# Identity products on TensorE in its first idle stretches, in an attention and MLP kernel

## The chip, the cores and the metric

The kernel runs on one core of one Trainium2 chip. The metric is device time in microseconds (us). Three runs of the kernel before gave 598.51, 599.78 and 601.29 us; the median is 599.78 us. One further execution was profiled: it took 598.44 us, of which the span from the first to the last instruction is 596.7 us and 1.7 us lie around it. All rows below come from that execution, and its times count from the start of its span.

## The reference

Attention with rotated queries and keys, then a two-layer MLP whose nonlinearity is a clipped parabola. Cut to what matters:

```python
# q, k, v: (4, 8, 576, 64); w_in: (512, 2048); w_out: (2048, 512); all float32
q_rot, k_rot = rotate(q), rotate(k)          # halves of the 64 turned by cos/sin of the position
scores = q_rot @ k_rot.transpose(0, 1, 3, 2) / 8
attn = exp(scores - max(scores))
attn = attn / (sum(attn) + 1e-9)
x = (attn @ v).transpose(0, 2, 1, 3).reshape(2304, 512)
h = x @ w_in
g = where(h >= 1, h, where(h <= -1, 0, (h + 1) ** 2 / 4))
out = g @ w_out                              # float32
```

## The kernel before

Each float32 operand of a large product is split into two float16 numbers, a high and a low part, after scaling by a power of two that is found at run time from a sum of squares; a product of two such operands is three float16 products. TensorE (PE) does the products, ScalarE (ACT) and VectorE (DVE) scale, split, exponentiate and reduce, SyncE (SP) issues all DMAs. Per batch element there are two blocks of 256 queries; a block runs over four pairs of heads and its scores, softmax, transposes by DMA, products with v and MLP steps are mixed with those of its neighbours.

What sets the order: every step is added to a `Plan` with its engine, and then all steps are issued in the order that the table `ORDER` gives. Each number of it is a position in the list of steps that are still left. Each engine works through its own instructions strictly in that order, so a step that waits holds up all that stand behind it on its engine. Steps on different engines wait for each other where their data ask for it.

The first 20 us, which the change touches, do this for the first batch element:

- `init` lets GpSimd (POOL) write the 128x128 float32 identity `idn` (it lies in the second half of the tile `xT`, by whose name the profile calls it) and then the permutation `prm`.
- k of each pair of heads comes by DMA into `rk`. ACT squares it with a running sum (L249). `root` lets PE add up that sum over the partitions (L255: all ones times one column, into `psV`), from which DVE takes an exponent in five or so tiny instructions (L260, L262, L265, L272).
- DVE turns k and q by the angles (L289, L291). `split_sum` (L318, L319) adds the two terms on PE: `idn` times `rk`, and `prm` times the other buffer (named `w` in the profile), into the two banks `psO`; for q into the bank `psH`. ACT takes the high part out of the bank (L327), PE subtracts it there (L323, with `nd`, a scaled identity), and ACT takes the low part.
- `scores` (L595) writes `psS`; DVE takes the row maximum (L568), ACT the exponential (L570).
- `prep_w` reads the words of w_in and w_out on DVE (L516, L518, L520) as soon as their DMAs have landed; its rest (L547, L548) is on PE.

A float32 product is recorded as two matmuls and two weight loads, so a row of the profile with x2 is one product of the program.

Of the kernel before, what the change touches and what calls it, by code (L numbers as in the profile page):

```python
# [1 line left out]

# [1 line left out]

# [16 lines left out]

ORDER = """
# [58 lines left out]
"""  # L83

PICK = set("""
lo0 lo12 lo15 m1.2 m1.6 m2.0 m2.1 m2.2 m2.3 m2.4 m2.7 m3.0 m3.1 m3.2 m3.3 m3.4 m3.5 m4.0 m4.1 m4.3 m5.2 m5.3
m5.4 m5.5 m6.0 m6.1 m6.2 m6.4 m6.5 m6.6 m6.7 m7.2 m7.4 m7.5 m8.2 m8.4 m8.5 m9.0 m9.1 m9.2 m9.3 v0 v1  # L90
""".split())
O_CHUNKS = 5


class Plan:
# [38 lines left out]
        self.steps.append((eng, cost, at, fn, sorted(deps.items()), f"{self.group} {eng}", bw, turn,  # L134
                           f"{self.group}.{self.part} {eng}", mode, self.alt))

    def order(self):
        left = list(range(len(self.steps)))
        return [self.steps[left.pop(int(k))][3] for k in ORDER.split()]


@with_exitstack
def kernel(
# [12 lines left out]
    nc = tc.nc  # L156
    B, _, NP, S = km.shape[1:]
# [43 lines left out]
    idn = x1[:, 2048:2304].bitcast(F32)  # L201
# [7 lines left out]
    psS = [ps.tile([128, 1024], F32, name=f"psS{i}") for i in range(2)]  # L209
# [637 lines left out]
                      [("xL", l, e, j) for l in range(2) for e in range(2) for j in range(NP)], 128,  # L847
                      [done + span * (m + nst + 0.5) for m in range(4)], left_rows(b - 1))

    order = plan.order()  # L850
    with tc.manual_schedule():
        for fn in order:
            fn()
# [57 lines left out]
```

## Time and profile before

| what | value |
|---|---|
| median of three runs | 599.78 us (598.51 to 601.29) |
| profiled execution | 598.44 us, span 596.7 us |
| PE busy | 564.8 us, 95% of the span |
| DVE busy | 482.3 us, 81% |
| ACT busy | 455.9 us, 76% |
| mean granted clock of PE | 0.991 |
| the chain that ended last, by engine | PE 64%, DVE 15%, ACT 10%, DMA 7%, issue 3%, SP 1% |

How to read it: the shares are averages over stages with different limits. PE is busy nearly all the time from 80 us on, but not in the first 60 us, where DVE and ACT are. A timeline row has the start, the length, the engine, the line of the kernel, the operation, what is written and read, its shape and how many instructions were merged; in brackets the idle time of the engine just before it and who ended it. The clock column is the share of TensorE's full 2.4 GHz that was granted. A matmul's end is modelled, so the spacing of starts tells more than the length.

### The profile page before, as it was taken

The numbers are of one execution on the slowest core, as the hardware profiler recorded it, in microseconds if no ns is written. First come the engines' busy times: TensorE is split into PE (matmuls) and PEld (weight loads), VectorE is DVE, ScalarE is ACT, GpSimd is POOL, SyncE is SP. The second block draws the span as 40 slices with busy tenths as digits, with TensorE's granted clock in tenths as the row PEclk, the third lists the DMA queues.
The fourth block names the chain that finished last, engine by engine and source line by source line (L and its number), as shares of the span: only waits on it lengthen the run. The fifth ranks groups of instructions, "written<-read, shape, count | busy, mean of one in ns | idle before, by whom it ended". The sixth has DMA issues, their size and how long they took to land.

```text
span 596.7 us, 12159 instructions
## 1 busy us (share of the span) xinstructions
PE 564.8 (95%) x4824; PEld 365.1 (61%) x4824; DVE 482.3 (81%) x782; ACT 455.9 (76%) x922; POOL 1.5 (0%) x11
## 2 busy tenths in 40 slices
PE   4758989899999999999999999999999999999996
PEld 3423556556576766666666666666577666676763
DVE  6999999999899999989999788778988765523332
ACT  4999989999899889896957778787887676452431
POOL 1000000000000000000000000000000000000000
PEclk9889989999999999999999999999999999999999
DMA  8999998967986899596856892672557547400001
GB/s 271 337 215 264 242 242 224 286 120 143 224 187 164 157 168 208 103 236 158 178 136 134 189 170 41 110 152 59 120 96 140 75 85 137 98 10 27 1 3 52
DMA packets 184008, 88.94 MB, mean 149 GB/s; under 512 B 170768, under 2 KB 172048, under 8 KB 183952
## 3 DMA queue, kind: packets, MB, share of 16 engines
q1 hardware_dynamic: 183952, 88.17, 66.7%
q8 instruction: 38, 0.62, 0.4%
q14 instruction: 18, 0.15, 0.1%
HBM read 38.60 MB, written 4.72 MB: 73 GB/s over the span
## 4 chain that ended last, share of the span: by engine, by line
PE 64%; DVE 15%; ACT 10%; DMA 7%; issue 3%; SPq 1%; DVEq 0%; ACTq 0%
PE psO L741 25%; PE psH L709 24%; PE psV L630 7%; PE psS L595 5%; DMA pT<-phl 3%; DVE phl L580 3%; DVE sca L568 3%; ACT p L570 2%; ACT phl L578 2%; DMA w<-in_w_out_dram 2%; DVE g L732 1%; PE psO L547 1%; DVE r L728 1%; DMA w<-in_w_in_dram 1%; DMA rk<-in_km_dram 1%
## 5 line engine op out<-in xcount | busy, mean ns | idle before, releaser
L709 PE MATMUL psH<-xT,w 128*128 128x256 f16 (+1 forms) x1920 | 205.3, 262 | 1.2 <-ACT a L717 1.2
L741 PE MATMUL psO<-w,g 128*128 128x512 f16 x864 | 203.4, 379 | 0.0
L709 PEld LDWEIGHTS <-w 128*128 128x128 f16 x1920 | 171.1, 98 | 36.9 <-issue 4.0
L741 PEld LDWEIGHTS <-g 128*128 128x128 f16 x864 | 81.5, 98 | 83.8 <-issue 2.8
L570 ACT ACTIVATE p<-psS,sca 128x576 f32<-128x576 f32 x144 | 105.5, 736 | 29.2 <-DVE sca L568 20.8
L580 DVE SCALAR_TENSOR_TENSOR phl<-p,sca,phl 128x576 f16<-128x576 f32 x144 | 115.8, 812 | 11.5 <-ACT phl L578 11.0
L578 ACT ACTIVATE phl<-p,sca 128x576 f16<-128x576 f32 x144 | 107.8, 770 | 16.0 <-DVE sca L575 11.5
L568 DVE TENSOR_REDUCE sca<-psS 128x1 f32<-128x576 f32 x144 | 105.3, 749 | 8.9 <-PE psS L595 8.1
L732 DVE SCALAR_TENSOR_TENSOR g<-r,g 128x512 f16<-128x512 f32 x72 | 49.4, 686 | 34.9 <-ACT g L730 34.7
L717 ACT ACTIVATE a<-psH 128x512 f32<-128x512 f32 x72 | 42.4, 589 | 41.8 <-PE psH L709 37.9
L728 DVE SCALAR_TENSOR_TENSOR r<-a,r 128x512 f32<-128x512 f32 x72 | 49.4, 686 | 20.3 <-ACT r L726 19.4
L730 ACT ACTIVATE g<-r 128x512 f16<-128x512 f32 x72 | 45.0, 625 | 23.2 <-DVE r L728 13.1
L595 PE MATMUL psS<-kT,qT 64*128 64x512 f16 (+1 forms) x768 | 59.7, 284 | 2.9 <-ACT p L570 2.7
L595 PEld LDWEIGHTS <-qT 64*128 64x128 f16 x768 | 29.2, 94 | 46.6 <-issue 24.2
L630 PE MATMUL psV<-pT,vS 128*64 128x256 f16 (+1 forms) x512 | 42.4, 288 | 1.7 <-DMA pT<-phl 1.7
L630 PEld LDWEIGHTS <-vS 128*64 128x64 f16 x512 | 26.8, 109 | 8.8 <-issue 5.9
L721 DVE SCALAR_TENSOR_TENSOR r<-a 128x512 f32<-128x512 f32 x38 | 26.1, 687 | 6.0 <-ACT a L717 5.2
L570 ACT ACTIVATION_READ_ACCUMULATOR p<-psS,sca 128x1 f32 x144 | 28.6, 199 | 0.0
L630 PE MATMUL psV<-pT,vM 128*64 128x256 f16 (+1 forms) x320 | 25.0, 286 | 0.0
L724 ACT ACTIVATE r<-a 128x512 f32<-128x512 f32 x34 | 21.2, 625 | 4.0 <-DVE g L732 2.1
L726 ACT ACTIVATE r<-r 128x512 f32<-128x512 f32 x34 | 21.3, 627 | 0.6
L644 DVE SCALAR_TENSOR_TENSOR xT<-psV,sca,xT 128x320 f16<-128x320 f32 (+1 forms) x24 | 14.6, 610 | 7.7 <-ACT xT L641 7.7
(108 smaller groups left out, 475.7 us busy)
## 6 DMA issues: line engine op xcount, KB each, us to landing
w<-in_w_in_dram SPq DMA_DIRECT2D x14, 512.0 KB, 6.6
w<-in_w_out_dram SPq DMA_DIRECT2D x12, 512.0 KB, 8.0
rv<-in_vm_dram SPq DMA_DIRECT2D x8, 512.0 KB, 4.5
out_dram<-o SPq DMA_DIRECT2D x16, 256.0 KB, 3.0
dup<-in_km_dram SPq DMA_DIRECT2D x6, 576.0 KB, 6.6
rk<-in_km_dram SPq DMA_DIRECT2D x6, 576.0 KB, 4.5
rq<-in_qb_dram SPq DMA_DIRECT2D x4, 640.0 KB, 5.0
vM<-vS SPq DMA_DIRECT2D x8, 256.0 KB, 5.3
```

The lines of the kernel that those rows point to most:

```text
L568: plan.add("dve", dve_cost(S, psum=True), at, lambda m=m, src=src: nc.vector.tensor_reduce(out=m, in_=src, op=ALU.max, axis=AX.X, negate=T ...
L570: plan.add("act", act_cost(S, psum=True, ptrs=2), at, lambda a=a, e=e, m=m, src=src: nc.scalar.activation(out=p32[e], in_=src, func=AF.Exp ...
L578: plan.add("act", act_cost(S), at, lambda a=a, e=e, hi=hi: nc.scalar.activation(out=hi, in_=p32[e], func=AF.Copy, scale=rr[:, a:a + 1]), r ...
L580: plan.add("dve", dve_cost(S, ptrs=1), at, lambda a=a, e=e, hi=hi, lo=lo: nc.vector.scalar_tensor_tensor(out=lo, in0=p32[e], scalar=rr[:, ...
L595: nc.tensor.matmul(out=psS[a][:, lo:hi], lhsT=qT[hf][d, l, j, c:c + 128], rhs=kT[ks][d, j, m, lo:hi], start=z == 0, stop=z == 2)
L630: nc.tensor.matmul(out=outs[a], lhsT=st, rhs=moving(a, blk), start=z == 0, stop=z == len(seq) - 1)
L709: nc.tensor.matmul(out=psH[:, n * i:n * i + n], lhsT=wi[ft // 2][:, wl, kk, 128 * (ft % 2):128 * (ft % 2) + 128], rhs=xfn(xl, kk), start=z ...
L717: plan.add("act", act_cost(512, psum=True, ptrs=0), at, lambda one=one: nc.scalar.activation(out=a, in_=psH, func=AF.Relu, scale=2.0 ** -7 ...
L728: plan.add("dve", dve_cost(512), at, lambda one=one: nc.vector.scalar_tensor_tensor(out=r, in0=a, scalar=one, in1=r, op0=ALU.max, op1=ALU. ...
L730: plan.add("act", act_cost(512, ptrs=0), at, lambda g=g, one=one: nc.scalar.activation(out=g[:, 0], in_=r, func=AF.Relu, scale=1.0, bias=- ...
L732: plan.add("dve", dve_cost(512), at, lambda g=g, one=one: nc.vector.scalar_tensor_tensor(out=g[:, 1], in0=r, scalar=-one, in1=g[:, 0], op0 ...
L741: nc.tensor.matmul(out=psO[pos[tt]], lhsT=g[:, gl, n * i + 128 * tt:n * i + 128 * tt + 128], rhs=wo[ft // 2][:, wl, ft % 2, :], start=ft = ...
```

## The change

Five entries of a new kind stand in `ORDER`: `*b.n` calls `idle(b, n)`, which issues n products of `idn` with itself into the first 128 columns of a PSUM bank (bank 0 is `psH`, bank 4 the first of `psS`). Nothing reads them; the next real product into that bank starts it anew. There are 7 + 6 + 5 + 7 products into `psH` and 2 into `psS`. All numbers of the table are the same as before and in the same order.

```diff
...
-5 4 4 9 1 2 26 4 1 0 0 75 48 51 25 122 121 98 22 46 70 3 25 21 3 129 128 91 91 1 2 4 3 2 2 17 0 16 13 17 55 31
-32 15 0 51 30 15 12 27 1 0 5 24 5 0 0 3 0 1 0 17 3 3 2 75 35 0 0 207 7 32 11 69 203 14 203 11 67 29 46 1 197 0
...
+5 4 4 *0.7 9 1 2 26 4 1 0 0 75 48 51 25 122 121 98 22 46 70 3 *0.6 25 21 3 129 128 91 91 1 2 4 3 2 2 17 0 16 13
+17 55 31 32 15 0 51 30 15 12 27 *0.5 1 0 5 *0.7 24 5 0 0 3 0 1 0 17 3 3 2 75 35 0 0 *4.2 207 7 32 11 69 203 14
...
-    def order(self):
+    def order(self, idle):
         left = list(range(len(self.steps)))
-        return [self.steps[left.pop(int(k))][3] for k in ORDER.split()]
+        return [partial(idle, *map(int, k[1:].split("."))) if k[0] == "*" else self.steps[left.pop(int(k))][3]
+                for k in ORDER.split()]
...
-    order = plan.order()
+    def idle(b, n):
+        bank = (psH, psO[0], psO[1], psV, psS[0], psS[1])[b]
+        for _ in range(n):
+            nc.tensor.matmul(out=bank[:, 0:128], lhsT=idn, rhs=idn, start=True, stop=True)
+
+    order = plan.order(idle)
...
```

On PE, at the very start of the program, these rows stood in the kernel before (`psV` is the bank of the root sums, `psO` the two banks of k, `xT_78` is `idn`; lines are those of each kernel's own file, 3 higher in the changed one):

```order
L255 MATMUL psV<-sca 128x1 x2
L318 MATMUL psO_107<-rk,xT_78 128x288
L319 MATMUL psO_107<-w,prm 128x288
L318 MATMUL psO_108<-rk,xT_78 128x288
L319 MATMUL psO_108<-w,prm 128x288
L255 MATMUL psV<-sca 128x1
L318 MATMUL psH<-rq_86,xT_78 128x256
L319 MATMUL psH<-w,prm 128x256
```

And these stand there now:

```order
L856 MATMUL psH<-xT_78 128x128 x7
L258 MATMUL psV<-sca 128x1
L856 MATMUL psH<-xT_78 128x128 x6
L258 MATMUL psV<-sca 128x1
L856 MATMUL psH<-xT_78 128x128 x5
L321 MATMUL psO_107<-rk,xT_78 128x288
L322 MATMUL psO_107<-w,prm 128x288
L321 MATMUL psO_108<-rk,xT_78 128x288
L322 MATMUL psO_108<-w,prm 128x288
L856 MATMUL psH<-xT_78 128x128 x7
L258 MATMUL psV<-sca 128x1
L321 MATMUL psH<-rq_86,xT_78 128x256
```

So four batches stand ahead of the first, the second and the third root sum and of the first k products; no real instruction has moved against another.

On PE, a little later, ahead of the first scores (`psS_103` is the first score bank, `nd_99` the scaled identity of q), the kernel before had:

```order
L323 MATMUL psH<-qT_64,nd_99 128x256
L595 LDWEIGHTS qT_64
L595 MATMUL psS_103<-kT_62,qT_64 128x512
```

And now:

```order
L326 MATMUL psH<-qT_64,nd_99 128x256
L856 MATMUL psS_103<-xT_78 128x128 x2
L598 LDWEIGHTS qT_64
L598 MATMUL psS_103<-kT_62,qT_64 128x512
```

The fifth batch stands between the subtraction of q and the first score product. The instructions of DVE, ACT, POOL and SP and their order are the same in both kernels.

## Rows read from the trace of the kernel before

**Rows 1.** The page's 40 slices: busy tenths of PE, DVE and ACT.

```profile
PE   4758989899999999999999999999999999999996
...
DVE  6999999999899999989999788778988765523332
ACT  4999989999899889896957778787887676452431
```

**Rows 2.** Chain that ended last, first 60 us: start us, us, what.

```profile
4.03 5.17 DMA rk<-in_km_dram
9.22 10.67 DMA w<-in_w_out_dram
...
19.99 0.69 DVE o L516
...
41.10 2.08 PE psO L547 x2
```

**Rows 3.** Timeline of PE.

```profile
5.87 0.59 PE L255 MATMUL psV<-sca 128*128 128x1 f32 x2 [5.87 <-ACT w L249]
7.78 0.59 PE L255 MATMUL psV<-sca 128*128 128x1 f32 x2 [1.32 <-ACT w L249]
9.42 1.30 PE L318 MATMUL psO<-rk,xT 128*128 128x288 f32 x2 [1.05 <-DVE sca L262]
...
11.47 1.17 PE L318 MATMUL psO<-rk,xT 128*128 128x288 f32 x2
12.43 1.17 PE L319 MATMUL psO<-w,prm 128*128 128x288 f32 x2
13.39 0.33 PE L255 MATMUL psV<-sca 128*128 128x1 f32 x2
...
14.10 0.59 PE L319 MATMUL psH<-w,prm 128*128 128x256 f32 x2
...
14.78 0.28 PE L255 MATMUL psV<-sca 128*128 128x1 f32 x2
...
16.04 0.85 PE L595 MATMUL psS<-kT,qT 64*128 64x512 f16 x10 [0.19 <-ACT kT L327]
...
17.41 0.65 PE L319 MATMUL psO<-w,prm 128*128 128x288 f32 x2
17.89 0.65 PE L318 MATMUL psO<-rk,xT 128*128 128x288 f32 x2
```

**Rows 4.** Timeline of DVE.

```profile
8.40 0.16 DVE L260 TENSOR_REDUCE sca<-psV 128x1 f32<-128x1 f32 x1
...
12.71 0.42 DVE L291 TENSOR_TENSOR rq<-rq,rt 128x256 f32<-128x256 f32 x1
...
15.03 0.69 DVE L516 TENSOR_SCALAR xT<-w 128x1024 uint32<-128x1024 uint32 x1 [0.31 <-DMA w<-in_w_in_dram]
...
16.92 0.76 DVE L568 TENSOR_REDUCE sca<-psS 128x1 f32<-128x576 f32 x1
...
19.99 0.69 DVE L516 TENSOR_SCALAR o<-w 128x1024 uint32<-128x1024 uint32 x1 [0.33 <-DMA w<-in_w_out_dram]
...
44.98 0.69 DVE L516 TENSOR_SCALAR o<-w 128x1024 uint32<-128x1024 uint32 x1 [1.41 <-PE psO L547]
```

**Rows 5.** Timeline of ACT.

```profile
13.63 0.50 ACT L327 ACTIVATE kT<-psO,sca 128x288 f16<-128x288 f32 x1 [1.06 <-PE psO L319]
14.73 0.47 ACT L327 ACTIVATE qT<-psH,sca 128x256 f16<-128x256 f32 x1 [0.60 <-PE psH L319]
...
17.71 0.74 ACT L570 ACTIVATE p<-psS,sca 128x576 f32<-128x576 f32 x1
```

**Rows 6.** Timeline of POOL: the identity.

```profile
1.01 0.29 POOL masks.py:199 TENSOR_SCALAR_AFFINE_SELECT xT<-xT 128x128 f32<-128x128 f32 x1
```

**Rows 7.** Timeline of the weight loads (PEld).

```profile
17.17 0.43 PEld L319 LDWEIGHTS psO<-w,prm 128*128 128x128 f32 x2
```

**Rows 8.** Stretches: busy of PE, PEld, DVE, ACT, POOL; PEclk, DMA share, GB/s.

```profile
10.00:13.40 3.40, 3.40 (x9) 2.37 (x8) 3.40 (x11) 2.53 (x7) 0.00 (x0) 1.00 0.99 331
...
25.00:27.20 2.20, 2.20 (x6) 1.47 (x6) 2.20 (x5) 2.01 (x8) 0.00 (x0) 0.51 0.99 331
...
40.50:44.20 3.70, 3.10 (x5) 1.35 (x6) 3.07 (x4) 3.38 (x9) 0.00 (x0) 0.54 1.24 246
```

More of the change, by code (lines that the diff above doesn't have):

```diff
@@ L1 @@
 from contextlib import ExitStack
+from functools import partial
 import numpy as np
```

112 rows, old and new, of the table ORDER are left out of this document.

## The prediction, made before the changed kernel ran

> **What bounds the kernel now.** I read the slices of the page first [rows 1]: PE is full only from about the sixth slice on (15 us each), while DVE is full from the second. So the first 60 us, where the change lies, are not PE's. Next the chain that ended last [rows 2]: it opens with the DMA that brings k (4.03 to 9.20 us), goes on with the DMA that brings w_out (9.22 to 19.89), and passes to DVE at 19.99, which waited for just that DMA. PE is not on it before 41.10 us. Then the timelines of PE, DVE and ACT beside each other [rows 3 to 5], to see who would notice a faster or a later PE in the first 20 us.
>
> PE runs there at its low rate at first. The product L318 or L319 of 288 columns starts 0.96 us after the one ahead at 11.47 and 12.43, and 0.48 us at 17.41 and 17.89 [rows 3]; the root sum L255 takes 0.59 us at 5.87 and 7.78, 0.28 us at 14.78. The granted clock reads 1.00 for 10.0 to 13.4 us [rows 8], which the doubled spacing contradicts, so for the start I go by the spacing: 1.2 GHz until about 13.4 us, 2.4 GHz after. Ahead of that rise PE had worked without a break since 9.42, 4.0 us; the two short root sums ahead of it lifted nothing. Two later falls are in the record (0.51 in 25.0 to 27.2, 0.54 in 40.5 to 44.2), and the second of these ended after 3.1 us of work in 3.7 [rows 8].
>
> **The change part by part.** No real instruction moves, and no engine but PE gets any. What is added is 27 products on PE, and what may go is the low rate from about 6 to 13.4 us.
>
> *Price of one product.* It is not in the trace. By columns, 128 of 288 of the nearest product give 0.96 x 128/288 = 0.43 us at the low rate and 0.48 x 128/288 = 0.21 at the high [rows 3]. The other end is that its two weight loads hide under nothing: L255, with one column, is hardly more than those loads, so 0.59 + 0.43 = 1.02 and 0.28 + 0.21 = 0.49. I take the lower end, because in the stream of float32 products the loads of L319 (17.17, 0.43 us) begin before its first column at 17.41 [rows 3, 7]. Less than the columns it cannot be.
>
> *Batch 1 (7).* It waits for the identity, ready at 1.01 + 0.29 = 1.30 [rows 6]. 7 x 0.43 = 3.0 us, done at 4.3. The root sum behind it waits for ACT until 5.87 in any case [rows 3]: 1.6 us of cover. Cost 0.
>
> *Batch 2 (6).* If PE has its high rate by then: the root sum is done at 5.87 + 0.28 = 6.15, the batch at 6.15 + 6 x 0.21 = 7.4, and the second root sum starts at 7.78 as before, on ACT [rows 3]. Cost 0, with 0.4 us of cover. Behind this batch stands the result for DVE's L260 at 8.40 [rows 4], which got it 0.03 us ahead of need (7.78 + 0.59 = 8.37); DVE is in order, so a later root sum holds all of DVE.
>
> *Batch 3 (5).* 8.06 + 1.07 = 9.1, ahead of 9.42, when DVE frees the first k product. Cost 0.
>
> *The four k products.* 4 x 0.48 = 1.9 instead of 4.0 us: they end at 11.35 instead of 13.39.
>
> *Batch 4 (7).* 11.35 + 1.5 = 12.85; the third root sum is done at 13.1 (before: 13.39 + 0.33). Turned q is there at 12.71 + 0.42 = 13.13 [rows 4], so the two products of q end at 13.13 + 0.43 + 0.59 = 14.15 (0.43 is 256 columns at the high rate) instead of 14.10 + 0.59 = 14.69. So 1.5 us of the 2.0 won go to the batch and to DVE.
>
> *Batch 5 (2).* 0.43 us between q and the scores. These ended at 16.04 + 0.85 = 16.89 [rows 3]; with q 0.54 earlier and the batch in full they end at 16.78, so DVE's maximum at 16.92 is not held. Cost 0, with 0.1 us of cover.
>
> *Who takes the gain.* ACT waits 1.06 us for k at 13.63 and 0.60 us for q at 14.73 [rows 5]; 1.06 and 0.54 of that go. But ACT's first exponential at 17.71 follows DVE's row maximum at 16.92 + 0.76, and DVE comes to that maximum straight from work that began at 15.03, when the DMA of w_in had landed [rows 4]. ACT would then idle about 1.6 us ahead of 17.71 instead of ahead of 13.63 and 14.73. At 19.99 DVE waits for the DMA of w_out, the chain's second link [rows 2, 4]. Nothing of a faster PE reaches 20 us, and from there on DVE, ACT and PE have what they had. The sum is 598.44 + 0 = 598.4 us.
>
> By the Trainium skill, "TensorE: Matmul & The Clock Gate", section "Terms", the penalty of a throttled clock is the throttled time times the share of pulses that is missing. For the k products alone that would give the 2.0 us back at the end, 596.4 us. The rows do not agree: the stretch is off the chain, so that rule prices PE's time and not the kernel's.
>
> *Against the median.* The profiled execution is 1.34 us under the median of the three runs, which lie 2.8 us apart. If part of that spread is the moment at which the rate rises at the start, the change narrows it; I can't show it from one trace and go half the way: 599.1 us.
>
> **The rivals.**
>
> *A. The first batch does not lift the rate.* Then batch 2 runs at 1.2 GHz: 6.46 + 6 x 0.43 = 9.0, the second root sum is done at 9.6, and DVE's L260 at 8.40 waits 1.2 us. From here it decides: any root sum done after 8.40 costs DVE time. If the rate rises after 4.0 us of work from 5.87 on, at 9.9, batch 3 ends at 10.8, the k products at 12.75, batch 4 at 14.25, the third root sum at 14.5, q at 15.55, 0.85 late; with batch 5 in full (0.43) the scores end at 16.89 + 1.28 = 18.2, 1.25 us after DVE wants them. 0.33 us of it vanish in the wait at 19.99 [rows 4]: + 0.9, 599.4 us. If only work without root sums lifts it (9.6 + 4.0 = 13.6), q ends 2.7 us late and the sum is + 2.8, 601.2 us. For it: batch 1 gives 3.0 us of work, a little less than what stood ahead of either rise in the rows. Against it: 3.1 us were enough once [rows 8].
>
> *B. The products' loads do not hide.* Price 1.02 and 0.49. With the rate up after 4.1 us, batch 1 ends at 6.9 (4 x 1.02 + 3 x 0.49), the second root sum at 10.4, batch 3 at 12.8, the k products at 14.75, batch 4 at 18.2, q at 19.5: 4.8 late, with batch 5 5.8 at the scores, less 0.33: + 5.5, 603.9 us. Against it stand rows 7.
>
> *C. PE's gain does pass.* If the order of DVE and ACT bends so that their 1.06 + 0.54 us count, 596.8 us. If besides the low rate at 40.5 to 44.2 falls away, on which DVE waits 1.41 us at 44.98 [rows 4, 8], 595.4 us. Against it: DVE waits for DMAs at 15.03 and 19.99, and what PE does at 37 to 41 us is set by ACT and DVE, which the change leaves as they are. The rule of the Trainium skill named above would put this rival at 596.4 us.
>
> **How the numbers follow.** My forecast 0.66, A 0.20, B 0.05, C 0.09. The time is that of the forecast, 599.1 us. The three runs tell a difference of about 0.5%, 3.0 us, from no change: under 596.8 is faster, over 602.8 slower. Faster is half of C and little else, 0.05; slower is B and a slow tail of A, 0.06; within is the rest, 0.89. For 8 in 10 the range takes the forecast with the spread of the runs, most of A and the near end of C: 597.2 to 601.8; B, the far end of C and the late end of A with a high run stay out.
>
> **What would show it.** Right: products 0.21 to 0.43 us apart; the k products 0.48 apart from about 9.4 on; the second root sum no later than 8.40; the third at 12.8; ACT with a new idle time of about 1.6 us ahead of its first exponential near 17.7; DVE still waiting for w_in near 15.0 and for w_out near 20.0; all rows after 20 us where they were. Wrong: DVE waiting for PE at L260 or at its first L568 (A, B); or DVE at L516 earlier than 19.9 (C). A change of more than 3 us with the first 20 us unmoved would mean that the later falls of the rate are set by something that I have not seen.

## The result

The changed kernel took 603.67 us (median of 9 runs, 601.04 to 604.29) against 600.17 us of the kernel before (9 runs, 598.07 to 601.29): a ratio of 1.0052, 95% interval 1.0036 to 1.0067. It is slower by about half a percent: 3.1 us by the ratio, while the medians lie 3.5 us apart. Three executions of 969 us or more, one each of e9, e11 and e12, are left out of the ratios below, but not out of the medians. I had forecast 599.1 us and no difference that can be told. The profiled execution took 604.29 us with a span of 602.5, against 598.44 and 596.7 before: 5.8 us, more than the typical 3.1, so this trace shows the loss in its larger form.

Lines of the changed file are 3 higher: L258 is the root sum, L263 its reduce on DVE, L321 and L322 the k and q products, L571 the row maximum, L519 the first step on a raw weight, L856 the identity products.

The timeline of PE in the changed kernel, where [rows 3] stood:

```profile
1.35 3.36 PE L856 MATMUL psH<-xT 128*128 128x128 f32 x14 [1.35 <-POOL xT masks.py:199]
5.80 0.59 PE L258 MATMUL psV<-sca 128*128 128x1 f32 x2 [1.09 <-ACT w L252]
6.25 2.91 PE L856 MATMUL psH<-xT 128*128 128x128 f32 x12
8.95 0.42 PE L258 MATMUL psV<-sca 128*128 128x1 f32 x2
9.23 2.06 PE L856 MATMUL psH<-xT 128*128 128x128 f32 x10
11.13 0.65 PE L321 MATMUL psO<-rk,xT 128*128 128x288 f32 x2
...
13.08 1.72 PE L856 MATMUL psH<-xT 128*128 128x128 f32 x14
14.64 0.28 PE L258 MATMUL psV<-sca 128*128 128x1 f32 x2
...
16.56 0.61 PE L856 MATMUL psS<-xT 128*128 128x128 f32 x4
17.10 0.98 PE L598 MATMUL psS<-kT,qT 64*128 64x512 f16 x12
```

Batch 2 goes from 6.25 to 8.95: 6 products 0.45 us apart, the low rate. The five of batch 3 take 1.90 us, so most of them are slow too; batch 4 (7 in 1.56 us, 0.22 each) and the k products are at the high rate. The rate rose near 10.9 us, neither by 6 us as I had forecast, nor as late as the 13.4 of before. The second root sum began at 8.95 instead of 7.78.

DVE's timeline shows who paid, where [rows 4] stood:

```profile
9.41 0.16 DVE L263 TENSOR_REDUCE sca<-psV 128x1 f32<-128x1 f32 x1 [1.12 <-PE psV L258]
...
18.11 0.76 DVE L571 TENSOR_REDUCE sca<-psS 128x1 f32<-128x576 f32 x1 [0.47 <-PE psS L598]
...
20.77 0.68 DVE L519 TENSOR_SCALAR o<-w 128x1024 uint32<-128x1024 uint32 x1
...
30.19 0.16 DVE L263 TENSOR_REDUCE sca<-psV 128x1 f32<-128x3 f32 x1 [1.23 <-PE psV L258]
31.87 0.16 DVE L263 TENSOR_REDUCE sca<-psV 128x1 f32<-128x3 f32 x1 [0.46 <-PE psV L258]
...
46.02 0.69 DVE L519 TENSOR_SCALAR o<-w 128x1024 uint32<-128x1024 uint32 x1
```

It waits 1.12 us for the second root sum and 0.47 us for the first scores, and reaches w_out at 20.77 instead of 19.99. Its two waits for DMAs there (0.31 and 0.33 us) are gone, which accounts for most of the lateness that disappears on the way. In this execution the two DMAs of w_out also landed sooner, 7.9 and 8.5 us after their issue instead of 9.2 and 10.7.

In the chain that ended last, DMAs stood in this place before [rows 2]; now the products do:

```profile
6.39 2.77 PE psH L856 x12
...
9.37 1.92 PE psH L856 x10
...
13.24 1.56 PE psH L856 x14
```

So far this is rival A. What I had not foreseen stands in the rows after it: two more waits, 1.23 and 0.46 us, for root sums at 30 us (their rows are in the fence above). The first profile of the kernel before has neither; its second (e6) has one of 0.74 us.

The clock goes with these. The low-rate stretches of the changed kernel (columns as in [rows 8]) are 6.8 us long each:

```profile
24.40:31.10 6.70, 5.97 (x19) 4.16 (x21) 5.47 (x14) 5.62 (x17) 0.00 (x0) 0.50 0.80 246
34.70:41.40 6.70, 5.78 (x17) 3.01 (x18) 6.70 (x18) 6.70 (x14) 0.00 (x0) 0.50 0.65 112
41.50:44.90 3.40, 1.78 (x14) 0.73 (x9) 3.40 (x6) 3.40 (x9) 0.00 (x0) 1.00 1.06 285
79.10:85.70 6.60, 5.18 (x29) 2.95 (x29) 6.60 (x10) 6.60 (x14) 0.00 (x0) 0.50 1.10 203
```

Those of the kernel before were 3.4 us each, the first and the last near the same places, the second 6 us later:

```profile
23.80:27.10 3.30, 3.14 (x8) 2.36 (x9) 3.30 (x6) 3.11 (x10) 0.00 (x0) 0.50 1.01 347
40.90:44.10 3.20, 3.00 (x5) 1.35 (x6) 2.67 (x4) 2.88 (x8) 0.00 (x0) 0.50 1.14 243
78.40:81.70 3.30, 3.30 (x6) 1.50 (x5) 3.30 (x4) 3.30 (x6) 0.00 (x0) 0.50 1.09 201
```

How the lateness runs through the program can be read from single rows of DVE, which has the same instructions in the same order in both kernels. The table gives the start of seven of them in the kernel before, and how much later (+) they start in the profiles of the other runs:

| row of DVE | reduce of 2nd root sum | first maximum | w_out, first step | maximum | w_out, second | w_in, third | last |
|---|---|---|---|---|---|---|---|
| before, us | 8.40 | 16.92 | 19.99 | 31.71 | 44.98 | 75.80 | 588.52 |
| changed | +1.01 | +1.19 | +0.78 | +2.54 | +1.04 | +4.08 | +5.81 |
| changed, again (e5) | +1.02 | +1.27 | +0.86 | +2.66 | +1.16 | +3.79 | +5.38 |
| before, again (e6) | -0.28 | +0.37 | -0.04 | +0.71 | +0.86 | +1.29 | +1.26 |
| batch 1 alone (e1) | -0.15 | -0.56 | -0.97 | +0.89 | -0.61 | -0.01 | -0.02 |
| batches 2, 3 (e2) | +0.99 | +0.58 | +0.16 | +0.98 | +1.13 | +1.00 | +1.49 |
| batches 4, 5 (e3) | -0.14 | +0.82 | +0.41 | +1.23 | +1.32 | +1.17 | +1.17 |
| DVE late (e4) | -0.08 | +0.63 | +0.21 | +0.66 | +0.68 | +1.24 | +1.12 |
| later idle (e7) | +0.14 | +0.93 | +0.53 | +0.50 | -0.99 | +1.73 | +2.85 |
| ten first (e8) | +0.17 | -0.30 | -0.72 | +0.04 | -1.45 | +0.96 | +1.01 |
| ten first, fill (e9) | -0.23 | -0.50 | -0.92 | -0.44 | -0.08 | -0.30 | +1.38 |
| changed, fill (e10) | +1.16 | +1.27 | +0.87 | +2.59 | +2.95 | +2.73 | +5.28 |
| before, fill (e11) | +0.46 | +1.14 | +0.73 | +1.49 | +1.85 | +1.94 | +2.50 |
| ten, 5, 4, 4, fill (e12) | -0.01 | -0.43 | -0.85 | -0.09 | +0.27 | +0.05 | +0.11 |

The second profile of the kernel before shows that a few tenths, and up to 1.3 us at the end, differ from execution to execution; the small entries of the table say no more than that. The steps of the changed kernel are larger than that and alike in its two profiles. They are: + 1.0 at the second root sum; + 1.8 between 20 and 31.7 us; - 1.5 at 45 us; + 3.0 between 46 and 80 us; and the rest later. The rest isn't one step: the row of DVE is 3.5 us late at 140 us, 5.0 at 280, 4.5 at 420 and 5.8 at 540, and no experiment follows it there.

The steps at 31.7 and 45 us belong to the low-rate stretches and not to the late start. The four profiles whose first stretch is a long one (the changed kernel's, e5, e10 and e1) have + 1.7 to + 1.9 us between 20 and 31.7; the others have at most + 0.8. In e1 no root sum of the start is late, it has the same + 1.86 and - 1.50, and its profile ends where that of the kernel before does.

The gain of 1.5 us at 45 us goes with the rate: PE is fast at 41.5 to 44.9 us in the changed kernel, and DVE's row at 46.02 has no wait, where that of before waited 1.41 us for PE [rows 4]. It is lost again at 73 to 78 us. ACT, changed kernel:

```profile
77.60 1.44 ACT L581 ACTIVATE phl<-p,sca 128x576 f16<-128x576 f32 x2 [3.57 <-DMA pT<-phl]
```

and the kernel before:

```profile
73.52 1.44 ACT L578 ACTIVATE phl<-p,sca 128x576 f16<-128x576 f32 x2 [0.71 <-DMA pT<-phl]
```

ACT writes into a buffer (`phl`) that a transpose by DMA still reads. The transposes stand in SyncE's queue one behind the other. Start and length of SyncE's instruction for the one issued near 57 us, before and after:

```profile
56.75 4.41 SPq L244 DMA_TRANSPOSE pT<-phl  x1
```

```profile
57.98 6.63 SPq L247 DMA_TRANSPOSE pT<-phl  x1
```

DVE and ACT had caught up 1.5 us at 45, the queue of transposes had not: the first of them was 2.54 us late (35.79 against 33.25 us), and the instruction at 57 took 2.2 us longer. The next transpose, the one that ACT waits for, was in flight for 8.05 us before and 10.67 us in the changed kernel (its rows in the two chains: `65.38 8.05 DMA pT<-phl` and `66.85 10.67 DMA pT<-phl`). Why the transposes take longer there is not shown.

### The profile page after: what moved, and what is told of

It is laid out like the page before. It is cut to its first block, busy times and chain, and to the rows that moved or that the text cites. A ratio compares the mean times of both kernels' runs of the same rounds, so it can differ in the third digit from the quotient of the medians.

```text
span 602.5 us, 12266 instructions
## 1 busy us (share of the span) xinstructions
PE 575.4 (96%) x4878; PEld 375.2 (62%) x4878; DVE 482.4 (80%) x782; ACT 455.0 (76%) x922; POOL 1.5 (0%) x11
## 4 chain that ended last, share of the span: by engine, by line
PE 69%; DVE 12%; ACT 9%; DMA 7%; issue 2%; SPq 0%; ACTq 0%; DVEq 0%
PE psO L744 26%; PE psH L712 25%; PE psV L633 8%; DMA pT<-phl 6%; PE psS L598 6%; DVE phl L583 3%; DVE sca L571 3%; ACT p L573 2%; PE psS L615 1%; ACT phl L581 1%; DVE g L735 1%; PE psH L856 1%; DVE r L731 1%; DVE o L523 1%; ACT w L532 1%
## 5 line engine op out<-in xcount | busy, mean ns | idle before, releaser
L571 DVE TENSOR_REDUCE sca<-psS 128x1 f32<-128x576 f32 x144 | 105.5, 751 | 10.3 <-PE psS L598 9.7
L733 ACT ACTIVATE g<-r 128x512 f16<-128x512 f32 x72 | 44.9, 624 | 23.2 <-DVE r L731 12.9
```

Source lines behind the costliest of these rows:

```text
L571: plan.add("dve", dve_cost(S, psum=True), at, lambda m=m, src=src: nc.vector.tensor_reduce(out=m, in_=src, op=ALU.max, axis=AX.X, negate=T ...
L733: plan.add("act", act_cost(512, ptrs=0), at, lambda g=g, one=one: nc.scalar.activation(out=g[:, 0], in_=r, func=AF.Relu, scale=1.0, bias=- ...
```

## The experiments

The theories: S, the loss is made at the start, where products at the low rate hold root sums and scores; F, it is made by the longer low-rate stretches after 20 us; W, it is the products as such; and, from e9 on, D, the pile at the transposes: what DVE and ACT win at 45 us they lose again waiting for SyncE's queue at 73 to 78. Ratios are to the kernel before in the same series.

**e1, batch 1 alone**

```diff
-5 4 4 9 1 2 26 ...
+5 4 4 *0.7 9 1 2 26 ...
```

> Only the first batch (7 products, ahead of the first root sum) is kept. Theory S (the start: the loss of the changed kernel comes from root sums and scores that the products make late while TensorE is at its low rate): the batch ends near 4.7 us, the root sum starts at 5.8 as before, nothing is late; the time is that of before, within 0.7 us. Theory F (the falls: the loss is made after 20 us, where the low rate lasts 6.8 us three times instead of 3.4 us): it too gives before, as nothing moves after 6 us. Theory W (the products as such, by the power or the activity they add, change what TensorE is granted later): a third of the loss or more, + 1 us.

Measured: 600.02 us, ratio 1.0012 (1.0000 to 1.0025). The batch ends at 4.7 us and the root sums are not late. The interval touches no change; a cost of 1 us is neither shown nor excluded, so W is not ruled out by this run alone. Three of its twelve runs have a mean granted clock of 0.982 and took 601.10 to 601.57 us, the other nine 598.28 to 600.34. Its profile has two long low-rate stretches and the two waits at 30 us (1.24 and 0.56), and still ends 0.02 us ahead of the kernel before:

```profile
22.90:29.60 6.70, 6.22 (x21) 4.16 (x23) 5.46 (x15) 5.63 (x18) 0.00 (x0) 0.50 0.95 319
33.10:39.80 6.70, 5.53 (x19) 3.05 (x20) 6.70 (x18) 6.70 (x14) 0.00 (x0) 0.50 0.68 114
```

**e2, batches 2 and 3 alone**

```diff
-... 46 70 3 25 21 3 ... 15 12 27 1 0 5 ...
+... 46 70 3 *0.6 25 21 3 ... 15 12 27 *0.5 1 0 5 ...
```

> Only the second and the third batch (6 and 5 products, ahead of the second root sum and of the first k products). Theory S: the second root sum is late by 1.1 to 1.2 us, DVE waits for it, and nearly all of the loss is there: + 2.5 to + 3.5 us. Theory F: the shift at 20 us is about the same 0.8 us, the total depends on how long the later low stretches last in each run: between + 0.5 and + 3.5 us, and runs with a higher mean granted clock lose less. Theory W: + 1 to + 1.5 us, by the number of products.

Measured: 600.14 us, ratio 1.0013 (1.0003 to 1.0024). DVE waits 1.30 us for the second root sum, as S said, but the loss is 0.8 us and not 2.5: most of the 0.99 is absorbed by 20 us (+ 0.16), and another 0.82 us comes in one wait at 29.16 us, much as in the kernel before in e6 (0.74). S as I had put it, with nearly all of the loss in this wait, falls.

**e3, batches 4 and 5 alone**

```diff
-... 1 0 5 24 5 ... 35 0 0 207 ...
+... 1 0 5 *0.7 24 5 ... 35 0 0 *4.2 207 ...
```

> Only the fourth and the fifth batch (7 ahead of the third root sum, 2 ahead of the first scores). The rate is low until about 13.4 us, as in the kernel before, so batch 4 starts there and holds the q products by 1.5 us at the high rate. Theory S: scores end 1.5 to 2 us late, + 1.5 us at 20 us and + 1.5 to + 4 us in the total. Theory F: the same shift at 20 us, the total by the length of the later low stretches. Theory W: + 1 us.

Measured: 601.01 us, ratio 1.0030 (1.0015 to 1.0045), the largest single part. Here the rate rises during the k products (the last is 0.49 us long by the spacing, the three ahead of it 0.89 to 1.09), and batch 4 starts behind them at 12.71 us:

```profile
12.71 1.73 PE L856 MATMUL psH<-xT 128*128 128x128 f32 x14
14.27 0.28 PE L258 MATMUL psV<-sca 128*128 128x1 f32 x2
```

There is little idle time at that place unless the k products are fast from their first; the batch stands ahead of the third root sum and q with its full 1.56 us. ACT waits 2.15 us for q (0.60 before [rows 5]), and DVE 0.53 us for the root sum and 0.48 us for the scores. The profiled execution took 599.64 us, 1.4 us less than the median, and ends no later than that of e6, so where the median's loss arises can't be read from it. The three parts add up to 0.12 + 0.13 + 0.30 = 0.55%, about the whole of the first series (0.52%), but twice what the changed kernel loses in e5 (0.28%).

**e4, DVE 1.1 us late, no product**

```diff
+    nc.vector.memset(a_s, 0.0)   # twice, ahead of the fourth turn of k (L294)
```

> No product on TensorE; instead two fills of an unused VectorE buffer (128x512 each, about 0.55 us each) right behind the second root sum's reduce, so that VectorE is 1.1 us late from 8.5 us on, as it is in the changed kernel. Theory S: the same loss from the same delay without any product: + 0.5 to + 0.8 us at 20 us, and + 2.5 to + 3.5 us in the total if the delay grows later as it did there, + 0.5 to + 0.8 us if it does not. Theory F: the total by the length of the later low stretches, so a spread with the granted clock. Theory W: before's time plus 0.5 us at most.

Measured: 599.73 us, ratio 1.0007 (0.9996 to 1.0018). The fills did not come where the expectation has them. In the trace they start 5 us behind the second root sum:

```profile
8.32 0.16 DVE L263 TENSOR_REDUCE sca<-psV 128x1 f32<-128x1 f32 x1
...
13.50 0.48 DVE L856 MEMSET a<- 128x512 f32 x1
14.16 0.48 DVE L856 MEMSET a<- 128x512 f32 x1 [0.17 <-DVE a L856]
...
15.17 0.15 DVE L263 TENSOR_REDUCE sca<-psV 128x1 f32<-128x1 f32 x1
```

So DVE is 1.1 us late from 13.5 us on and not from 8.4, and this delay is worth 0.2 us at 20 us and no loss that can be told at the end. A late DVE from the second root sum on, as in the changed kernel, was not tested without products; e2, which has it, loses 0.8 us.

**e5 and e6, the changed kernel and the kernel before once more**

No edit.

> The changed kernel once more, for a second profile and more runs beside the others. Theory S (the late root sum and scores at the start make the loss): + 3 to + 3.5 us, and the row of VectorE is about 1.0 us late from the second root sum on in this profile too. Theory F (later low-rate stretches of doubled length make the loss): a profile whose low stretches are single shows a loss of 1 us or less at the end, one with three double ones 4 to 6 us.

> The kernel before once more, for a second profile of it. All theories: the time of before within 0.4 us. Theory F: its low-rate stretches are not tied to the same moments, so one or two of the three may last 6.8 us here, and then the row of VectorE is late by 1 to 2 us behind it, as in the changed kernel. Theory S: they stay at 3.4 us.

Measured: e5 601.15 us, ratio 1.0028 (1.0012 to 1.0043); e6 599.19 us, 1.0000 (0.9990 to 1.0010). The second profile of the changed kernel has the same three long stretches as the first; that of the kernel before has four, all short ones. Over both series the 21 runs of the changed kernel fall in two groups by mean granted clock: the 7 at 0.982 took 603.67 to 604.29 us, the 14 at 0.983 to 0.994 took 598.36 to 602.46, mean 600.84. The 105 runs of the kernel before beside the experiments lie between 597.65 and 601.31 us, at 0.981 to 0.991. So the longest runs go with the long stretches, as F has it, but they are a third of all, and the first series had caught five of nine. F does not account for the mean: the twelve runs of e5 have a mean granted clock of 0.988, the same as the 35 of the kernel before in that series, and lose 1.7 us. S is missed too: it had + 3 to + 3.5 us, though DVE's row is 1.02 us late from the second root sum on, as it said. No profile of the changed kernel with short stretches alone came, so the half of F's expectation that rests on one is open.

**e7, products in the later idle stretches instead**

```diff
+    # into psV: 9 ahead of v's root sum, then 7, 4, 2 and 6 in the idle stretches up to 41 us
```

> None of the five batches; instead products into the free bank of the root sums in the idle stretches of TensorE between 21 and 41 us (9, 7, 4, 2 and 6 products, each batch shorter than its idle stretch at the high rate: 9 x 0.21 = 1.9 of 2.4 us and so on). They keep TensorE at work where the rate fell in the kernel before. Theory F: the low stretches at 24 and 41 us go, with them the 1.4 us that VectorE waits at 45 us, and the time falls by 1 to 2 us. Theory S: the start is that of before, nothing on the path changes: within 0.7 us of before.

Measured: 598.85 us, ratio 1.0002 (0.9985 to 1.0018): no gain. In its profile the clock does what was wanted, and there is no fall between 15 and 76 us:

```profile
15.10:76.30 61.20, 51.12 (x329) 29.96 (x329) 57.51 (x106) 57.16 (x126) 0.00 (x0) 1.00 1.01 260
76.60:83.20 6.60, 5.02 (x29) 2.95 (x29) 6.60 (x10) 6.60 (x15) 0.00 (x0) 0.51 1.14 208
```

DVE is 0.99 us ahead at 45 us, and 1.73 behind at 75.8: ACT waits 3.3 us for the transposes, PE idles 4 us meanwhile, and its rate falls for 6.6 us. F's forecast of 1 to 2 us gained falls for the mean. But the runs lie in two groups, seven at 597.14 to 598.91 us and five at 600.47 to 601.99, and the profile is one of the second (601.31). The first group is some 1.2 us under the kernel before; that the transposes take the gain is seen for the second group alone.

**e8, ten products first, the other batches as in the change**

```diff
-5 4 4 *0.7 9 1 2 26 ...
+5 4 4 *0.10 9 1 2 26 ...
```

> The changed kernel with 10 instead of 7 products in the first batch: 10 x 0.43 = 4.3 us of work from 1.35 to 5.6 us, right up to the first root sum, so that TensorE works without a gap. Theory S: the rate is up during batch 2 or before it in more of the runs, the second root sum is late by 0.5 us or less, and the loss shrinks to + 1 to + 2 us (batch 4 stays). Theory F: nothing at 24 us and later knows of this; + 3 to + 3.5 us as in the changed kernel.

Measured: 599.46 us, ratio 0.9996 (0.9983 to 1.0009). The loss is gone. PE's timeline:

```profile
1.35 4.08 PE L856 MATMUL psH<-xT 128*128 128x128 f32 x20 [1.35 <-POOL xT masks.py:199]
5.89 0.38 PE L258 MATMUL psV<-sca 128*128 128x1 f32 x2 [0.46 <-ACT w L252]
6.14 1.58 PE L856 MATMUL psH<-xT 128*128 128x128 f32 x12
8.07 0.38 PE L258 MATMUL psV<-sca 128*128 128x1 f32 x2 [0.35 <-ACT w L252]
...
9.51 0.69 PE L321 MATMUL psO<-rk,xT 128*128 128x288 f32 x2
...
11.49 1.72 PE L856 MATMUL psH<-xT 128*128 128x128 f32 x14
13.05 0.28 PE L258 MATMUL psV<-sca 128*128 128x1 f32 x2
```

Batch 2 is at the high rate and ends ahead of the second root sum; the k products start at 9.51 and end by 11.5, batch 4 fits behind them. On PE this is my forecast step for step, with all 27 products of the change and three more in front. F, which had + 3 us here, falls, and so does W, as there are more products and no loss; S had + 1 to + 2 us, too much. Two low stretches of 6.8 us (32.0 and 76.4 us) stand in this profile too, and its two runs at a mean clock of 0.981 and 0.983 took 600.23 and 600.40 us, some 3.6 us less than the changed kernel's at 0.982. Two runs are few, but with the three of e1 (601.10 to 601.57) they point to a cost of the long stretches that is high only together with a late start.

**e9, e8 with a fill on DVE at 45 us**

```diff
+    nc.vector.memset(a_s, 0.0)   # three times, ahead of the L519 step at 45 us
```

> The kernel of the run with ten first products, plus three fills of an unused VectorE buffer (about 1.6 us) ahead of the step at 45 us on which VectorE had waited 1.4 us for TensorE in the kernel before, and had not waited there. Theory D (the pile: where that wait is gone, VectorE and ACT run 1.5 us ahead of SyncE's queue, loads and copies go out among the transposes, and ACT then waits 2.7 to 3.6 us instead of 0.5 to 1.2 for the transposes at 73 to 78 us): with the fill ACT waits about 1 us there, VectorE's row is late by + 0.1 at 47 us and by no more than + 0.8 at 75 us, and the time is that of before or up to 1 us less, in spite of 1.6 us of added work. Rival S (only the start counts): VectorE stays 1.6 us later than without the fill, so + 1 to + 1.6 us.

Measured: 599.72 us, ratio 0.9999 (0.9984 to 1.0015). The fills take 1.7 us in the trace, and they cost nothing that can be told. ACT at the transposes, in e8 and in e9:

```profile
74.48 1.44 ACT L581 ACTIVATE phl<-p,sca 128x576 f16<-128x576 f32 x2 [2.73 <-DMA pT<-phl]
```

```profile
72.91 1.44 ACT L581 ACTIVATE phl<-p,sca 128x576 f16<-128x576 f32 x2 [0.25 <-DMA pT<-phl]
```

DVE's row goes from - 1.45 to + 0.96 between 45 and 75.8 us without the fill, from - 0.08 to - 0.30 with it. D is shown for these two profiles: what is won at 45 us is lost at the transposes. Rival S of this run (+ 1 to + 1.6 us) falls.

**e10, the changed kernel with the same fill; e11, the kernel before with it**

```diff
+    nc.vector.memset(a_s, 0.0)   # three times, at the place of e9
```

> The changed kernel plus the same fills. Theory D: the step from + 1.0 to + 4.1 us that the changed kernel's VectorE row makes between 70 and 75 us shrinks to under 1 us, and the time falls by 0.5 to 1.5 us against the changed kernel: + 0.5 to + 1.5 us against before. Rival S: the fill adds to the loss, + 3 to + 5 us.

> The kernel before plus the same fills. Where VectorE waits 1.4 us there, the fill takes the place of the wait and costs 0.2 us; in executions in which the rate is high at 41 to 44 us it does what that wait did. Theory D: within 0.4 us of before, and less spread. Rival S: + 0.2 to + 1.6 us.

Measured: e10 601.36 us, ratio 1.0029 (1.0016 to 1.0043), as e5's 1.0028; e11 600.13 us, 1.0007 (0.9992 to 1.0021). In e10's profile the step between 46 and 80 us is gone (+ 2.95 to + 2.73), as D said, and ACT waits for no transpose; but the total is no better. The fill itself kept DVE at + 2.95 where it had come back to + 1.04, and the rest is lost further on: DVE's row is at + 1.84 at 140 us and + 4.46 at 160, where transposes hold ACT again (1.11 us in the kernel before, 2.07 in the changed one) and PE's rate falls for 3.4 us:

```profile
154.15 0.78 ACT L581 ACTIVATE phl<-p,sca 128x576 f16<-128x576 f32 x1 [2.42 <-DMA pT<-phl]
```

D's mechanism holds at 73 to 78 us, its forecast of the total doesn't: removing that pile doesn't remove the loss. e11 fits D (within 0.4 us of before) and S (+ 0.2 to + 1.6) alike, and its spread, 597.89 to 601.24 us, is not less than that of before.

**e12, ten first, then 5, 4 and 4, with the fill**

```diff
-*0.7 ... *0.6 ... *0.5 ... *0.7 ... *4.2
+*0.10 ... *0.5 ... *0.4 ... *0.4 ... (the fill of e9)
```

> Ten products first, then 5, 4 and 4 (none before the scores), with the fills: the rate up early, no root sum and no score late. Theory S and D together: VectorE is 0.3 to 0.9 us earlier than before at 20 us and not later at 75 us; the time is 0 to 1 us under before. If only the length of the later low stretches counts (theory F), the time is before's within 0.7 us, with a spread of 3 us or more.

Measured: 599.93 us, ratio 1.0010 (0.9995 to 1.0025). Nothing is late in its profile, and nothing is gained: S and D together had 0 to 1 us under before, of which the interval leaves 0.3. That the runs are spread by 5 us about the time of before (597.93 to 602.93) F had too. No version here beats the kernel before.

## Why the prediction was wrong

- **What bounds the start** was right for one execution only. In the profile that I read, DVE waited for the DMA of w_out, and PE was off the chain until 41.10 us. In the second profile of the same kernel (e6) the two DMAs of w_out landed 7.4 and 8.0 us after their issue instead of 9.2 and 10.7 (`DMA to landing us min/median/max: 7.4/7.7/8.0`), DVE waits for neither, and the chain goes over PE's slow products:

```profile
7.50 0.60 PE psV L255 x2
8.23 0.76 DVE rk L291
9.14 1.30 PE psO L318 x2
...
13.53 1.06 PE psH L318 x2
...
16.41 0.89 PE psS L595 x10
17.31 0.76 DVE sca L568
```

DVE waits there 0.43 us for a root sum and 0.48 us for the scores. That the DMAs hid PE's low rate was the luck of the first profile. That a fast PE gains nothing held all the same: with it (e8) DVE reaches its first maximum at 16.62 us and w_out at 19.27, 0.3 and 0.7 us earlier, without waiting for a DMA, and the time is that of before. One sign did not come: ACT has no idle time ahead of its first exponential (17.40 in e8), but waits 1.43 us for q at 14.34, which batch 4 holds back.
- **The price of a product** was right: 0.45 us or a little less at the low rate (batch 2) and 0.22 at the high (batch 4) against 0.43 and 0.21. The loads hide; rival B falls.
- **Batch 2** is the step that failed: "If PE has its high rate by then". It hadn't. I took 3.0 us of work for enough since 3.1 had been once; in that row the work stood closer together than here, where 1.1 us of idle time follows. With ten products (4.1 us of work and 0.46 idle) the rate was up before batch 2. In the other two profiles with ten first the rise comes a little later: e9's six products of batch 2 take 1.42 us, nearly the high rate, e12's five 1.81 us, so some of those are slow; in all three of the changed kernel's order (the first, e5, e10) batch 2 is slow throughout, 2.70 us. I gave 0.66 to the forecast, which hangs on this condition, and 0.20 to rival A, in which it fails; the failure deserved the larger chance.
- **Rival A's place and price** were right as far as 20 us: a wait of 1.2 us forecast and 1.12 measured, + 0.9 us forecast and + 0.78 measured.
- **Batch 4** hangs on the same condition. I priced it at nothing behind fast k products that begin at 9.42. In the changed kernel they begin at 11.13, and batch 4 ends at 14.64, 1.25 us after the third root sum stood before; behind k products at the low rate it costs 0.30% together with batch 5 (e3).
- **"From there on DVE, ACT and PE have what they had"** was wrong, and it set the range: A's upper end was 601.2 us. I carried a delay to the end as it was at 20 us. In the profile of the changed kernel it is 2.5 us at 31.7, as PE's low-rate stretch lasts 6.8 instead of 3.4 us and DVE waits for two root sums in it, 4.1 us behind the transposes at 75.8, and 5.8 us at the end. The rate's falls were in my rows, and I treated their lengths as fixed.
- **Rival C** (a faster PE passes its gain on) falls on its main count, e8, and on its second, e7: the 1.41 us at 45 us can be had, and in the profiles the transposes take them back. The Trainium skill's rule of the throttled time ("TensorE: Matmul & The Clock Gate", section "Terms") would give half of the two low stretches that e7 removed, an estimate of 3.4 us or 0.57%; less the half of the 3.4 us by which e7's stretch at 77 us is longer, it is 1.7 us or 0.28%. The measurement decides: e7's interval (0.15% faster to 0.18% slower) excludes both.

What stays open: why a given execution has long or short low-rate stretches, and how a start that is 1 us late becomes a loss of 1.3 us and more at the end, since neither the long stretches (e1) nor the pile at 73 to 78 us (e10) do it alone. Times of one and the same kernel lie up to 5.5 us apart in a series (e5), the shares of the runs at 0.982 differed between the series (5 of 9, 2 of 12), and no experiment held the moment of the falls fixed. How the mean loss of 0.3 to 0.5% divides between the late start and the long stretches is therefore known only roughly: about 1.3 us in the 14 runs outside 0.982, some 4 us in the others.

## What to carry to other kernels

Work that is put into an idle stretch is free only if it is short enough at the rate that the engine really has there; price it at the low rate, and look at what stands behind it in order on the same engine and who waits for that. Warm-up work belongs where nothing waits behind it, and in one piece: three more products in front turned a loss of 0.3 to 0.5% into none, though they gained nothing either. A change that moves PE or DVE earlier by 1 or 2 us can lose it again at a queue further on (here the transposes): ask which queue the gain will run into. And a wait of 0.3 us in one profile is no bound yet: take a second profile of the kernel before, and see whether the same engine waits for the same thing.

## What the runs showed of the hardware

- A float32 product of 128 columns with the identity, one behind the other, takes 0.22 us at 2.4 GHz (batch 4) and 0.45 at 1.2 GHz (batch 2); with 288 columns it is 0.48 and 0.96, so the columns set the time and the weight loads hide.
- Each low-rate stretch after 20 us, in all 14 profiles, lasted either 3.4 or 6.8 us. In a long one PE was busy 5.97 of 6.70 us and still had the low rate.
- The moment at which the rate first rises is not fixed. The second profile of the kernel before (e6) has its first q product, 0.51 us long by the spacing in the first profile (13.59 to 14.10), still at 1.00 us (13.39 to 14.39):

```profile
13.39 1.20 PE L318 MATMUL psH<-rq,xT 128*128 128x256 f32 x2
14.39 0.68 PE L319 MATMUL psH<-w,prm 128*128 128x256 f32 x2
```

The Trainium skill says as much ("TensorE: Matmul & The Clock Gate", section "Part 1: The HAM clock gate"): how many products at a kernel's start are slow differs from run to run.

- The profile's clock column can't be trusted ahead of the first rise: it reads 1.00 for 6.30 to 8.90 us of the changed kernel, where the products are 0.45 us apart. The mean granted clock of a run says nothing of the start either: the 0.991 of the kernel before is what its three later stretches alone give (half of 10.2 us in 596.7).
- SyncE's instruction for one transpose by DMA took 4.41 us in the kernel before and 6.63 us in the changed one, for the same bytes, and the transpose landed 6.4 and 8.7 us after its start. The order of SyncE's queue is the same in both; what makes the difference is not shown.
